# The sum of phi(k) moves from Pool to a column-tiled batch on PE, layernorm is applied six tiles behind, and each output tile starts with its attention part

## The chip, the core and the metric

The kernel runs on one core of a Trainium2 chip. The metric is the device time in microseconds of one execution, as a median over runs. Engines are named as in the profile: PE (matrix multiply), PEld (its weight loads), DVE (vector), ACT (activation), POOL (GpSimd), SP (issues most of the DMA).

## The reference

x has 2048 rows (positions) of 512 features, in bf16. Attention has 32 heads of 16 features. One gate value per row mixes the two branches.

```
g = sigmoid((x * gate_w).sum(-1, keepdims=True))
# branch A, linear attention
q, k, v = split_heads(x @ wqkv)
phi = lambda t: where(t > 0, t + 1, exp(t)) + 1e-6
pq, pk = phi(q), phi(k)
kv = einsum("bhsd,bhse->bhde", pk, v);  z = einsum("bhsd->bhd", pk)
a = merge_heads((pq @ kv) / (pq . z + 1e-6)) @ wo
# branch B, token-mixing MLP on h = layernorm(x) over the features
u = gelu(einsum("bsd,sf->bdf", h, w1) + b1)       # F = 1792
b = transpose(einsum("bdf,fs->bds", u, w2) + b2)
out = g * a + (1 - g) * b
```

## The kernel before

The 2048 rows are 16 tiles of 128. The program is one fixed order per engine: each engine takes its instructions in the order in which the code issues them, and waits on semaphores where operands come from another engine or from a DMA. All PSUM tiles come from one pool of 8 banks of 128x512 fp32; a bank is reused when its last reader is done.

- **K stage** (lines 252 to 272, to about 47 us). For each tile t: `k_tiles` multiplies the transposed tile by the k weights (4 matmuls into `kacc`); `phi` makes phi(k) from it with an Exp on ACT (`e`), a min-and-add on DVE (`e` in place) and a max-and-add on DVE (`pk`). A POOL add then sums `pk` into `zacc` (line 211), which later gives z. `g_tile(t-2)` adds x^T phi(k) of an earlier tile into four banks `gacc` (4 matmuls); kv follows from it and the v weights later. Tiles 0 to 7 are transposed on PE (4 small matmuls each) and copied to `xT` by DVE or ACT; tiles 8 to 15 come transposed by DMA. Beside this runs the layernorm of branch B: `ln_stats` (two DVE instructions per tile, `stats` and `mv`); for each group of four tiles `ln_rstd` (a DVE add `veps`, a POOL power `rstd`) and `ln_shift` (DVE, `nmr`); and `ln_apply` (one ACT instruction per tile writes `hs`). `ln_apply` runs four tiles behind: that of tile 0 stands on ACT behind the Exp of tile 4 and ahead of those of tiles 5 and later.
- **q stage** (lines 332 to 345, to about 78 us). Sixteen steps: 3 matmuls of `uacc` (the first three column blocks of w1) and 4 of `qacc`, whose phi is again one ACT and two DVE instructions. The last tiles of `ln_apply` and the evictions of `gacc` to `gT` run at its start. Inside stand `kv_matmuls` (step 4; it also turns `zacc` into the columns `Z32` that the denominator needs) and `w2_matmuls` (step 8).
- **u stage** (to about 114 us): the other 11 column blocks of w1, 16 matmuls each. `den_matmuls` (16 matmuls of 32 columns, on four column groups of the array), a reciprocal, and a chain of DMAs and DVE multiplications that scales `pqT`.
- **Output stage** (lines 393 to 415): for each row tile 14 matmuls of branch B (`yps`), ACT scales them by 1 - g and adds the bias (`b_sc`), 4 matmuls of branch A (`aps`), and DVE adds g times these (`ot`); SP stores the tile. The last tile's attention part goes in two halves of 256 columns.

Of the kernel before, what the change touches and what calls it, by code (L numbers as in the profile page):

```python
# [15 lines left out]
def kernel(  # L16
# [13 lines left out]
    nc = tc.nc  # L30
    P = nc.NUM_PARTITIONS
# [27 lines left out]
    work = ctx.enter_context(tc.tile_pool(name="work", bufs=3))  # L59
# [17 lines left out]
    pqT = keep([P, ND, S], BF16, "pqT")  # L77
    pk = keep([P, NT, D], BF16, "pk")
    uT = keep([P, NF, D], BF16, "uT")
    kvbdT = keep([P, ND, P], BF16, "kvbdT")  # L80
    W2sb = keep([P, ND, D], BF16, "W2sb")
    Z32 = keep([P, ND, 32], BF16, "Z32")
    zacc = keep([P, D], FP32, "zacc")
    zcol = keep([P, ND], FP32, "zcol")
    rden = keep([P, SC], BF16, "rden")
    ident = keep([P, P], BF16, "ident")
# [11 lines left out]
    gg = keep([P, NT], FP32, "gg")  # L98
    c1 = keep([P, NT], FP32, "c1")
    c2 = keep([P, NT], FP32, "c2")  # L100
    mhalf = keep([P, TPC], FP32, "mhalf")
    ones_f = keep([P, 1], FP32, "ones_f")
    warm = keep([P, SC], BF16, "warm")

    def mm(o, lhsT, rhs, start, stop, **kw):
        nc.tensor.matmul(o, lhsT=lhsT, rhs=rhs, start=start, stop=stop, **kw)  # L106
# [56 lines left out]
    )  # L163
    block_mask(mask[:].rearrange("p (a b) -> p a b", b=HEAD), P // HEAD, HEAD)
    block_mask(maskH[:].rearrange("p (a b) -> p a b", b=1), 8, 1)
    nc.gpsimd.memset(zacc[:], 0.0)
    nc.gpsimd.dma_start(out=brow[0:NF, :], in_=B_b1.rearrange("(f q) -> f q", q=P))
    nc.gpsimd.dma_start(out=brow[NF : NF + NT, :], in_=B_b2.rearrange("(f q) -> f q", q=P))
    nc.gpsimd.dma_start(
        out=gw_b[:], in_=gate_w.rearrange("(o d) -> o d", o=1).to_broadcast([P, D])  # L170
# [12 lines left out]
    def transpose_tile(t, on_act):  # L183
        pt = bank("pt", BF16)
        for k in range(ND):
            nc.tensor.transpose(pt[:, k * P : (k + 1) * P], xs[:, t, k * P : (k + 1) * P], ident[:])
        dst = xT[:, :, t * P : (t + 1) * P]
        src = pt[:].rearrange("p (k s) -> p k s", k=ND)
        if on_act:
            nc.scalar.activation(out=dst, in_=src, func=ACT.Copy)  # L190
        else:
            nc.vector.tensor_copy(out=dst, in_=src)
# [8 lines left out]
            out=dst, in0=acc[:], scalar=0.0, in1=e[:], op0=ALU.max, op1=ALU.add  # L201
        )

    def k_tiles(ts):
        accs = [bank("kacc") for _ in ts]
        for k in range(ND):
            for t, acc in zip(ts, accs):
                mm(acc[:], xT[:, k, t * P : (t + 1) * P], wk_sb[:, k, :], k == 0, k == ND - 1)
        for t, acc in zip(ts, accs):
            phi(pk[:, t, :], acc)  # L210
            nc.gpsimd.tensor_tensor(out=zacc[:], in0=zacc[:], in1=pk[:, t, :], op=ALU.add)  # L211

    def ln_stats(t):
        stats = work.tile([P, nc.vector.BN_STATS_DIM], FP32, name="stats", tag="stats", bufs=2)
        nc.vector.bn_stats(out=stats[:], in_=xs[:, t, :])  # L215
        nc.vector.bn_aggr(out=mv[:, t, :], in_=stats[:])  # L216

    def ln_rstd(g):
        s = slice(g * TPC, (g + 1) * TPC)
        nc.vector.tensor_scalar_add(out=veps[:, s], in0=mv[:, s, 1], scalar1=EPS)  # L220
        nc.gpsimd.tensor_tensor(out=rstd[:, s], in0=veps[:, s], in1=mhalf[:], op=ALU.pow)  # L221

    def ln_shift(g):
        s = slice(g * TPC, (g + 1) * TPC)
# [13 lines left out]
    def g_tile(t):  # L238
        for k in range(ND):
            mm(gacc[k][:], xs[:, t, k * P : (k + 1) * P], pk[:, t, :], t == 0, t == NT - 1)  # L240

    def q_block(i):
        c, j = divmod(i, ND)
        qacc = bank("qacc")
        for k in range(ND):
            mm(
                qacc[:], wq_sb[:, k, j * P : (j + 1) * P], xT[:, k, c * SC : (c + 1) * SC],
                k == 0, k == ND - 1,
            )
        phi(pqT[:, j, c * SC : (c + 1) * SC], qacc)  # L250

    transpose_tile(0, False)
    transpose_tile(1, False)
    warm_up(2, 256)
    k_tiles((0, 1))
    transpose_tile(2, True)
    transpose_tile(3, True)
    LAG = 2
    for t in range(2, NT + LAG):
        if t < NT:  # L260
            k_tiles((t,))
        if 4 <= t + 2 < 8:
            transpose_tile(t + 2, True)
        g_tile(t - LAG)
        if t % TPC == 0 and t <= NT:
            ln_shift(t // TPC - 1)
        if TPC <= t:
            ln_apply(t - TPC)
        for u in (0, 1, 2) if t == 2 else (t,) if t < NT else ():
            ln_stats(u)  # L270
            if u % TPC == TPC - 1:
                ln_rstd(u // TPC)

    gT = persist.tile([P, ND, D], BF16, name="gT", tag="wk_sb")
    for k in range(ND):
        if k % 2:
            nc.vector.tensor_copy(out=gT[:, k, :], in_=gacc[k][:])
        else:
            nc.scalar.activation(out=gT[:, k, :], in_=gacc[k][:], func=ACT.Copy)
    for t in range(NT + LAG - TPC, NT):  # L280
        ln_apply(t)

    def gelu(j, acc):
        nc.scalar.activation(  # L284
# [9 lines left out]
    def kv_matmuls():  # L294
        kvps = bank("kvps")
        for j in range(ND):
            for k in range(ND):
                mm(
                    kvps[:, j * P : (j + 1) * P], wv_sb[:, k, j * P : (j + 1) * P],
                    gT[:, k, j * P : (j + 1) * P], k == 0, k == ND - 1,  # L300
                )
        nc.vector.tensor_tensor(
            out=kvbdT[:], in0=kvps[:].rearrange("p (j d) -> p j d", j=ND),
            in1=mask[:].unsqueeze(1).to_broadcast([P, ND, P]), op=ALU.mult,
        )
        zps = bank("zps")
        for j in range(ND):
            mm(zps[:, j : j + 1], zacc[:, j * P : (j + 1) * P], ones_f[:], True, True)
        nc.vector.tensor_copy(out=zcol[:], in_=zps[:, 0:ND])
        for j in range(ND):  # L310
            nc.vector.tensor_scalar_mul(
                out=Z32[:, j, 8 * j : 8 * j + 8], in0=maskH[:], scalar1=zcol[:, j : j + 1]
            )
# [51 lines left out]
    w2c = []  # L365
# [6 lines left out]
    for j in range(NB0, NF):  # L372
        c, jj = divmod(j, FB)
# [18 lines left out]

    for t in range(NT):
        c, tl = divmod(t, TPC)
        yps = bank("yps")
        for f in range(NF):
            mm(yps[:], w2c[c][:, f, tl * P : (tl + 1) * P], uT[:, f, :], f == 0, f == NF - 1)
        b_sc = work.tile([P, D], FP32, name="b_sc", tag="b_sc", bufs=2)
        nc.scalar.activation(  # L399
            out=b_sc[:], in_=yps[:], func=ACT.Identity,  # L400
            scale=c1[:, t : t + 1], bias=c2[:, t : t + 1],
        )
        halves = 2 if t == NT - 1 else 1
        W = D // halves
        for h in range(halves):
            cs = slice(h * W, (h + 1) * W)
            aps = bank("aps")
            for j in range(ND):
                mm(aps[:, :W], pqT[:, j, t * P : (t + 1) * P], W2sb[:, j, cs], j == 0, j == ND - 1)
            ot = opool.tile([P, D], BF16, name="ot", tag="ot")  # L410
            nc.vector.scalar_tensor_tensor(  # L411
                out=ot[:, :W], in0=aps[:, :W], scalar=gg[:, t : t + 1], in1=b_sc[:, cs],
                op0=ALU.mult, op1=ALU.add,
            )
            nc.sync.dma_start(out=o_view[:, t, cs], in_=ot[:, :W])

# [29 lines left out]
```

## Time and profile before

| What | Value |
|---|---|
| median of 3 runs (lowest, highest) | 183.13 us (183.01, 184.39) |
| the profiled execution | 182.21 us, span 180.2 us |
| mean granted TensorE clock | 0.987 |
| busy: PE, DVE, ACT, POOL | 165.0, 89.5, 57.5, 36.9 us |

The span runs from the first to the last instruction that the profiler saw; the rest of the 182.21 us lies around it. A granted clock of 1.00 is the higher of TensorE's two levels, 2.4 GHz, and 0.50 the lower, 1.2 GHz. Matmul ends are modelled, so pitches (start to start) are used for matmul durations.

### The profile page before, as it was taken

What the parts mean: (1) busy time and instruction counts of PE and PEld (TensorE: products, weight loads), DVE (VectorE), ACT (ScalarE), POOL (GpSimd) and SP (SyncE); (2) the same over time, 40 slices, a digit from 0 to 9 for tenths busy, and PEclk for the clock granted to TensorE, in tenths of its full rate; (3) what the DMA queues carried; (4) which work ended last, traced back from release to release, by engine and by line L of the source; (5) the groups of instructions that cost most, each with busy time, mean ns of one, the idle gap of its engine ahead of it and who ended that gap; (6) DMA issues with size and microseconds to landing.
All of it is one profiled execution on the core that took longest, in us unless ns stands there. A gap on an engine that the chain in (4) does not pass through costs nothing.

```text
span 180.2 us, 2109 instructions
## 1 busy us (share of the span) xinstructions
PE 165.0 (92%) x792; PEld 74.6 (41%) x792; DVE 89.5 (50%) x192; ACT 57.5 (32%) x90; POOL 36.9 (20%) x53
## 2 busy tenths in 40 slices
PE   7799597884799999999999999999999999999991
PEld 3354133331346444444444444444444444444440
DVE  1489898988739787699901141204411111311111
ACT  3442745527192323561121131103311122111121
POOL 7275454574500000000063234200000000000000
PEclk9999969999999999999999999999999999999998
DMA  5999999996000000029019949996211000011100
GB/s 154 334 206 230 363 349 348 347 338 161 0 0 4 2 0 0 0 77 328 6 62 284 253 128 298 235 308 156 87 33 60 30 29 29 29 33 50 38 29 29
DMA packets 27866, 24.53 MB, mean 136 GB/s; under 512 B 5648, under 2 KB 27280, under 8 KB 27856
## 3 DMA queue, kind: packets, MB, share of 16 engines
q1 hardware_dynamic: 25984, 21.63, 40.9%
q0 software_dynamic: 1440, 2.38, 5.7%
q10 hardware_dynamic: 432, 0.39, 0.7%
q8 instruction: 6, 0.10, 0.3%
q14 instruction: 4, 0.03, 0.1%
HBM read 21.11 MB, written 2.23 MB: 130 GB/s over the span
## 4 chain that ended last, share of the span: by engine, by line
PE 70%; DVE 17%; ACT 4%; DMA 2%; POOL 2%; issue 1%; SPq 0%; DVEq 0%
PE yps L106 27%; PE uacc L106 26%; PE qacc L106 7%; PE aps L106 7%; DVE stats L215 4%; DVE pk L200 4%; DVE e L197 3%; DMA wk_sb<-in_A_wqkv_dram 2%; POOL rstd L221 2%; ACT e L196 2%; DVE nmr L225 2%; DVE mv L216 1%; ACT hs L231 1%; DVE veps L220 1%; PE kacc L106 1%
## 5 line engine op out<-in xcount | busy, mean ns | idle before, releaser
L106 PE MATMUL uacc<-hs,w1c 128*128 128x512 bf16 x224 | 51.3, 379 | 0.0
L106 PE MATMUL yps<-uT,w2c 128*128 128x512 bf16 x224 | 51.0, 379 | 0.0
L106 PEld LDWEIGHTS <-w2c 128*128 128x128 bf16 x224 | 21.9, 98 | 26.5
L106 PEld LDWEIGHTS <-w1c 128*128 128x128 bf16 x224 | 21.8, 98 | 26.2 <-issue 0.4
L411 DVE SCALAR_TENSOR_TENSOR ot<-aps,gg,b_sc 128x512 bf16<-128x512 f32 (+1 forms) x17 | 12.1, 719 | 40.9 <-PE aps L106 36.7
L399 ACT ACTIVATE b_sc<-yps,c,c 128x512 f32<-128x512 f32 x16 | 12.3, 777 | 49.0 <-PE yps L106 39.4
L106 PE MATMUL gacc<-pk,xs 128*128 128x512 bf16 x64 | 17.3, 394 | 6.4 <-DVE pk L200 6.3
L211 POOL TENSOR_TENSOR zacc<-zacc,pk 128x512 f32<-128x512 f32 x16 | 18.4, 1153 | 20.5 <-DVE pk L200 20.4
L106 PE MATMUL kacc<-wk_sb,xT 128*128 128x512 bf16 x64 | 17.4, 395 | 3.3 <-ACT xT L190 3.1
L363 DVE TENSOR_TENSOR pqT<-pqT,rex 128x512 bf16<-128x512 bf16 x16 | 6.7, 425 | 27.3 <-DMA rex<-rd_dram 27.2
L231 ACT ACTIVATE hs<-xs,nmr,rstd 128x512 bf16<-128x512 bf16 x16 | 12.7, 809 | 18.2 <-DVE nmr L225 18.2
L197 DVE TENSOR_SCALAR e<-e 128x512 bf16<-128x512 bf16 x32 | 12.5, 391 | 11.9 <-ACT e L196 11.9
L284 ACT ACTIVATE uT<-uacc,bcol 128x512 bf16<-128x512 f32 x14 | 9.3, 687 | 28.6 <-PE uacc L106 28.6
L106 PE MATMUL qacc<-xT,wq_sb 128*128 128x512 bf16 x64 | 16.4, 379 | 0.4 <-DVE pqT L200 0.2
L106 PE MATMUL aps<-W2sb,pqT 128*128 128x512 bf16 (+1 forms) x68 | 16.4, 367 | 0.0
L196 ACT ACTIVATE e<-qacc 128x512 bf16<-128x512 f32 x16 | 9.2, 597 | 13.8 <-PE qacc L106 12.9
L361 POOL DMA_DIRECT2D rex<-rd_dram x16 | 9.4, 594 | 16.6 <-DVE pqT L363 14.8
L106 PEld LDWEIGHTS <-xs 128*128 128x128 bf16 x64 | 6.2, 100 | 15.0 <-issue 9.8
L196 ACT ACTIVATE e<-kacc 128x512 bf16<-128x512 f32 x16 | 9.3, 588 | 7.0 <-PE kacc L106 7.0
L200 DVE SCALAR_TENSOR_TENSOR pk<-kacc,e 128x512 bf16<-128x512 f32 x16 | 11.1, 692 | 0.6
L200 DVE SCALAR_TENSOR_TENSOR pqT<-qacc,e 128x512 bf16<-128x512 f32 x16 | 11.1, 692 | 0.6
L106 PEld LDWEIGHTS <-xT 128*128 128x128 bf16 x64 | 6.2, 101 | 11.9 <-ACT xT L190 3.8
(61 smaller groups left out, 87.4 us busy)
## 6 DMA issues: line engine op xcount, KB each, us to landing
w2c<-in_B_w_dram SPq DMA_DIRECT2D x4, 1792.0 KB, 10.8
w1c<-in_B_w_dram SPq DMA_DIRECT2D x2, 2048.0 KB, 16.9
w1c<-in_B_w_dram SPq DMA_DIRECT2D x3, 1024.0 KB, 9.2
rex<-rd_dram POOLq DMA_DIRECT2D x16, 128.0 KB, 6.9
out_dram<-ot SPq DMA_DIRECT2D x15, 128.0 KB, 1.7
xs<-in_A_x_dram SPq DMA_DIRECT2D x3, 512.0 KB, 8.1
wq_sb<-in_A_wqkv_dram SPq DMA_DIRECT2D x1, 512.0 KB, 4.4
wv_sb<-in_A_wqkv_dram SPq DMA_DIRECT2D x1, 512.0 KB, 11.2
```

What stands on the lines that cost most here:

```text
L106: nc.tensor.matmul(o, lhsT=lhsT, rhs=rhs, start=start, stop=stop, **kw)
L196: nc.scalar.activation(out=e[:], in_=acc[:], func=ACT.Exp)
L197: nc.vector.tensor_scalar(out=e[:], in0=e[:], scalar1=1.0, scalar2=PHI_EPS, op0=ALU.min, op1=ALU.add)
L200: nc.vector.scalar_tensor_tensor(out=dst, in0=acc[:], scalar=0.0, in1=e[:], op0=ALU.max, op1=ALU.add)
L211: nc.gpsimd.tensor_tensor(out=zacc[:], in0=zacc[:], in1=pk[:, t, :], op=ALU.add)
L215: nc.vector.bn_stats(out=stats[:], in_=xs[:, t, :])
L231: nc.scalar.activation(out=hs[:, t, :], in_=xs[:, t, :], func=ACT.Identity, scale=rstd[:, t : t + 1], bias=nmr[:, t : t + 1],)
L284: nc.scalar.activation(out=uT[:, j, :], in_=acc[:], func=ACT.Gelu_apprx_tanh, bias=bcol[:, j : j + 1])
L361: nc.gpsimd.dma_start(out=rex[:], in_=src.unsqueeze(1).to_broadcast([8, HEAD, SC]))
L363: nc.vector.tensor_tensor(out=seg, in0=seg, in1=rex[:], op=ALU.mult)
L399: nc.scalar.activation(out=b_sc[:], in_=yps[:], func=ACT.Identity, scale=c1[:, t : t + 1], bias=c2[:, t : t + 1],)
L411: nc.vector.scalar_tensor_tensor(out=ot[:, :W], in0=aps[:, :W], scalar=gg[:, t : t + 1], in1=b_sc[:, cs], op0=ALU.mult, op1=ALU.add,)
```

## The change

1. The 16 POOL adds into `zacc` (and its memset) go. Instead a new `z_tile(t)` multiplies `pk` of tile t by a 128x32 matrix `zsel`, whose first column is ones, in one of four column groups of the array; the 16 of them stand at the end of the K stage, 15 ahead of the last `g_tile` and one behind it. DVE copies the result to `zsb`, which takes the place of `zacc`.
2. `ln_apply` goes six tiles behind in place of four, `ln_shift` is issued a tile later and behind `ln_stats` of its tile, and the layernorm of tiles 12 to 15 moves into the q stage (statistics in steps 2 to 5, apply in steps 8 to 11). The statistics of tiles 0 and 1 move ahead of the first `k_tiles`.
3. Tiles 2 and 3 are transposed and copied ahead of the first phi, tile 2 by DVE and not by ACT.
4. In the output stage the attention part comes first: `aps`, then ACT writes `a_sc` (scaled by g, with the bias), then `yps`, and DVE adds 1 - g times these. The last tile splits `yps` and not `aps` in halves.

```diff
-            nc.gpsimd.tensor_tensor(out=zacc[:], in0=zacc[:], in1=pk[:, t, :], op=ALU.add)
+    def z_tile(t):
+        g = t % 4
+        mm(
+            zacc[32 * g : 32 * g + 32, :], zsel[:], pk[:, t, :], t < 4, t >= NT - 4,
+            tile_position=(0, 32 * g),
+        )
...
-    k_tiles((0, 1))
-    transpose_tile(2, True)
-    transpose_tile(3, True)
+    ln_stats(0)
+    ln_stats(1)
+    k_tiles((0, 1), lambda: (transpose_tile(2, False), transpose_tile(3, True)))
     LAG = 2
-    for t in range(2, NT + LAG):
-        if t < NT:
-            k_tiles((t,))
+    APPLY = 6
+    for t in range(2, NT):
+        k_tiles((t,))
         if 4 <= t + 2 < 8:
             transpose_tile(t + 2, True)
         g_tile(t - LAG)
-        if t % TPC == 0 and t <= NT:
+        if t >= APPLY:
+            ln_apply(t - APPLY)
+        if t < 12:
+            ln_stats(t)
+            if t % TPC == TPC - 1:
+                ln_rstd(t // TPC)
+        if t % TPC == 1 and t > TPC:
             ln_shift(t // TPC - 1)
...
+    zacc = bank("zacc")
+    g_tile(NT - 2)
+    for t in range(NT - 1):
+        z_tile(t)
+    g_tile(NT - 1)
+    z_tile(NT - 1)
+    ln_apply(10)
+    ln_apply(11)
+    nc.vector.tensor_copy(out=zsb[:], in_=zacc[:])
...
         q_block(t)
+        if 2 <= t < 6:
+            ln_stats(t + 10)
+        if t == 5:
+            ln_rstd(3)
+        if t == 7:
+            ln_shift(3)
+        if 8 <= t < 12:
+            ln_apply(t + 4)
```

Where the instructions stand on the engines, in three places.

ACT, the start of the K stage, before (`e<-kacc` is the Exp of a tile, `xT<-pt` the copy of a transposed tile, `hs` an `ln_apply`):

```order
L196 ACTIVATE e<-kacc 128x512 x2
L190 ACTIVATE xT<-pt 128x4x128 x2
L196 ACTIVATE e<-kacc 128x512
L190 ACTIVATE xT<-pt 128x4x128
L196 ACTIVATE e<-kacc 128x512
L190 ACTIVATE xT<-pt 128x4x128
L196 ACTIVATE e<-kacc 128x512
L190 ACTIVATE xT<-pt 128x4x128
L231 ACTIVATE hs<-xs,nmr,rstd 128x512
L196 ACTIVATE e<-kacc 128x512
L190 ACTIVATE xT<-pt 128x4x128
```

and now:

```order
L192 ACTIVATE xT<-pt 128x4x128
L198 ACTIVATE e<-kacc 128x512 x3
L192 ACTIVATE xT<-pt 128x4x128
L198 ACTIVATE e<-kacc 128x512
L192 ACTIVATE xT<-pt 128x4x128
L198 ACTIVATE e<-kacc 128x512
L192 ACTIVATE xT<-pt 128x4x128
L198 ACTIVATE e<-kacc 128x512
L192 ACTIVATE xT<-pt 128x4x128
L198 ACTIVATE e<-kacc 128x512
L234 ACTIVATE hs<-xs,nmr,rstd 128x512
```

The copy of tile 3 now stands ahead of the first Exp, the copy of tile 2 is gone from ACT, and the first `hs` stands behind the last copy (tile 7) and not ahead of it.

DVE, from the third-last tile to the end of the K stage, before:

```order
L200 SCALAR_TENSOR_TENSOR pk_80<-kacc_443,e_448 128x512
L215 BN_STATS stats_458<-xs_72 128x6
L216 BN_AGGR mv_94<-stats_458 128x2
L197 TENSOR_SCALAR e_466<-e_466 128x512
L200 SCALAR_TENSOR_TENSOR pk_80<-kacc_461,e_466 128x512
L215 BN_STATS stats_476<-xs_72 128x6
L216 BN_AGGR mv_94<-stats_476 128x2
L197 TENSOR_SCALAR e_484<-e_484 128x512
L200 SCALAR_TENSOR_TENSOR pk_80<-kacc_479,e_484 128x512
L215 BN_STATS stats_494<-xs_72 128x6
L216 BN_AGGR mv_94<-stats_494 128x2
L220 TENSOR_SCALAR veps_95<-mv_94 128x4
```

and now:

```order
L202 SCALAR_TENSOR_TENSOR pk_80<-kacc_426,e_431 128x512
L228 SCALAR_TENSOR_TENSOR nmr_98<-mv_95,rstd_97 128x4
L199 TENSOR_SCALAR e_446<-e_446 128x512
L202 SCALAR_TENSOR_TENSOR pk_80<-kacc_441,e_446 128x512
L199 TENSOR_SCALAR e_460<-e_460 128x512
L202 SCALAR_TENSOR_TENSOR pk_80<-kacc_455,e_460 128x512
L291 COPY zsb_85<-zacc_469 128x512
L296 CAST gT_497<-gacc_161 128x512
L296 CAST gT_497<-gacc_163 128x512
```

The statistics of the last four tiles are gone from between the phi of the tiles, and the copy `zsb` stands ahead of the evictions of `gacc`.

POOL, from the first DMA to the chain that scales `pqT`, before:

```order
L167 DMA brow<-in_B_b_dram 14x128
L168 DMA brow<-in_B_b_dram 16x128
L169 DMA gw_b<-in_gate_w_dram 128x512
L211 TENSOR_TENSOR zacc<-zacc,pk 128x512 x4
L221 TENSOR_TENSOR rstd<-veps,mhalf 128x4
L211 TENSOR_TENSOR zacc<-zacc,pk 128x512 x4
L221 TENSOR_TENSOR rstd<-veps,mhalf 128x4
L211 TENSOR_TENSOR zacc<-zacc,pk 128x512 x4
L221 TENSOR_TENSOR rstd<-veps,mhalf 128x4
L211 TENSOR_TENSOR zacc<-zacc,pk 128x512 x4
L221 TENSOR_TENSOR rstd<-veps,mhalf 128x4
L356 DMA rd_dram<-rden 128x512
```

and now:

```order
L169 DMA brow<-in_B_b_dram 14x128
L170 DMA brow<-in_B_b_dram 16x128
L171 DMA gw_b<-in_gate_w_dram 128x512
L224 TENSOR_TENSOR rstd<-veps,mhalf 128x4 x4
L381 DMA rd_dram<-rden 128x512
```

Only the four powers are left on POOL between the first loads and that chain.

## Rows read from the trace of the kernel before

**Rows 1.** Windows: start:end, us, busy of PE, PEld, DVE, ACT, POOL, granted clock, DMA.

```profile
9.70:47.20 37.50, 28.94 (x132) 12.28 (x130) 33.45 (x67) 17.96 (x30) 20.17 (x19) 0.95 0.97 278
47.20:78.50 31.30, 30.90 (x162) 14.55 (x161) 22.52 (x52) 15.73 (x26) 1.38 (x2) 1.00 0.00 1
```

**Rows 2.** Timeline of PE: start, us, instruction, count, idle before and releaser.

```profile
20.81 1.04 PE L106 MATMUL kacc<-wk_sb,xT 128*128 128x512 bf16 x4 [2.15 <-ACT xT L190]
26.83 1.03 PE L106 MATMUL gacc<-pk,xs 128*128 128x512 bf16 x4
...
28.55 1.03 PE L106 MATMUL gacc<-pk,xs 128*128 128x512 bf16 x4
...
41.97 1.02 PE L106 MATMUL gacc<-pk,xs 128*128 128x512 bf16 x4 [1.81 <-DVE pk L200]
...
47.18 0.81 PE L106 MATMUL uacc<-hs,w1c 128*128 128x512 bf16 x3
...
49.67 1.02 PE L106 MATMUL qacc<-xT,wq_sb 128*128 128x512 bf16 x4 [0.18 <-DVE gT L277]
```

**Rows 3.** Timeline of DVE in the K stage.

```profile
23.42 0.69 DVE L215 BATCH_NORM_STATS2 stats<-xs 128x6 f32<-128x512 bf16 x1
...
24.23 0.71 DVE L197 TENSOR_SCALAR e<-e 128x512 bf16<-128x512 bf16 x1
24.98 0.69 DVE L200 SCALAR_TENSOR_TENSOR pk<-kacc,e 128x512 bf16<-128x512 f32 x1
25.59 0.68 DVE L215 BATCH_NORM_STATS2 stats<-xs 128x6 f32<-128x512 bf16 x1
...
26.91 0.28 DVE L197 TENSOR_SCALAR e<-e 128x512 bf16<-128x512 bf16 x1
```

**Rows 4.** Timeline of POOL in the same stretch.

```profile
23.64 1.15 POOL L211 TENSOR_TENSOR zacc<-zacc,pk 128x512 f32<-128x512 f32 x1 [1.02 <-DVE pk L200]
25.81 1.15 POOL L211 TENSOR_TENSOR zacc<-zacc,pk 128x512 f32<-128x512 f32 x1 [1.02 <-DVE pk L200]
```

**Rows 5.** The tile e on DVE, 50 to 75 us: duration ns minimum/median/maximum.

```profile
L197 DVE TENSOR_SCALAR e<-e x15: 283/294/296, 53.3 to 74.3; 128x512 bf16<-128x512 bf16 x15
```

**Rows 6.** Timelines at the start: PE, PEld and ACT.

```profile
7.02 0.62 PE L186 MATMUL pt<-ident,xs 128*128 128x128 bf16 x8
...
9.34 0.33 PEld L186 LDWEIGHTS <-xs 128*128 128x128 bf16 x4 [0.21 <-DMA xs<-in_A_x_dram]
...
6.96 1.08 ACT L196 ACTIVATE e<-kacc 128x512 bf16<-128x512 f32 x2 [3.27 <-PE kacc L106]
7.93 1.09 ACT L190 ACTIVATE xT<-pt 128x512 bf16<-128x512 bf16 x2
```

**Rows 7.** Timeline of PE around the denominator's batch.

```profile
78.48 1.05 PE L106 MATMUL denps<-pqT,Z 128*32 128x512 bf16 x16
79.46 2.77 PE L106 MATMUL uacc<-hs,w1c 128*128 128x512 bf16 x12
```

**Rows 8.** The first loads of w1 on SP, and the page's median time to landing.

```profile
15.57 1.12 SPq L148 DMA_DIRECT2D w1c<-in_B_w_dram  x2
...
w1c<-in_B_w_dram SPq DMA_DIRECT2D x3, 1024.0 KB, 9.2
```

**Rows 9.** Timeline of PE behind w2_matmuls.

```profile
65.01 1.02 PE L106 MATMUL qacc<-xT,wq_sb 128*128 128x512 bf16 x4 [0.23 <-DVE pqT L200]
```

**Rows 10.** Timelines at the end: PE, ACT and DVE.

```profile
172.28 3.19 PE L106 MATMUL yps<-uT,w2c 128*128 128x512 bf16 x14
175.31 1.04 PE L106 MATMUL aps<-W2sb,pqT 128*128 128x256 bf16 x8
...
175.51 0.78 ACT L399 ACTIVATE b_sc<-yps,c,c 128x512 f32<-128x512 f32 x1 [3.11 <-PE yps L106]
...
176.32 0.88 DVE L411 SCALAR_TENSOR_TENSOR ot<-aps,gg,b_sc 128x256 bf16<-128x256 f32 x2 [3.03 <-ACT b_sc L399]
```

**Rows 11.** Windows: the stretch at the lower clock.

```profile
21.90:25.20 3.30, 3.30 (x9) 1.18 (x8) 3.16 (x8) 1.97 (x5) 1.88 (x2) 0.50 1.11 351
```

More of the change, by code (lines that the diff above doesn't have):

```diff
@@ L82 @@
     Z32 = keep([P, ND, 32], BF16, "Z32")
-    zacc = keep([P, D], FP32, "zacc")
+    zsb = keep([P, D], FP32, "zsb")
+    zsel = keep([P, 32], BF16, "zsel")
     zcol = keep([P, ND], FP32, "zcol")
@@ L158 @@
     nc.vector.memset(Z32[:], 0.0)
+    nc.vector.memset(zsel[:], 0.0)
+    nc.vector.memset(zsel[:, 0:1], 1.0)
     nc.gpsimd.memset(ident[:], 0.0)
@@ L165 @@
     block_mask(maskH[:].rearrange("p (a b) -> p a b", b=1), 8, 1)
-    nc.gpsimd.memset(zacc[:], 0.0)
     nc.gpsimd.dma_start(out=brow[0:NF, :], in_=B_b1.rearrange("(f q) -> f q", q=P))
@@ L202, in phi, with k_tiles @@
         )
-    def k_tiles(ts):
+    def k_tiles(ts, between=None):
         accs = [bank("kacc") for _ in ts]
@@ L208, in k_tiles @@
                 mm(acc[:], xT[:, k, t * P : (t + 1) * P], wk_sb[:, k, :], k == 0, k == ND - 1)
+        if between:
+            between()
         for t, acc in zip(ts, accs):
             phi(pk[:, t, :], acc)
-            nc.gpsimd.tensor_tensor(out=zacc[:], in0=zacc[:], in1=pk[:, t, :], op=ALU.add)
     def ln_stats(t):
@@ L264 @@
         g_tile(t - LAG)
-        if t % TPC == 0 and t <= NT:
-            ln_shift(t // TPC - 1)
[L267 to L272, printed above, removed]
+        if t >= APPLY:
[5 more added lines that the diff above has]
+        if t % TPC == 1 and t > TPC:
+            ln_shift(t // TPC - 1)
+    zacc = bank("zacc")
[7 more added lines that the diff above has]
+    nc.vector.tensor_copy(out=zsb[:], in_=zacc[:])
     gT = persist.tile([P, ND, D], BF16, name="gT", tag="wk_sb")
@@ L279 @@
             nc.scalar.activation(out=gT[:, k, :], in_=gacc[k][:], func=ACT.Copy)
-    for t in range(NT + LAG - TPC, NT):
-        ln_apply(t)
     def gelu(j, acc):
@@ L307, in kv_matmuls @@
         for j in range(ND):
-            mm(zps[:, j : j + 1], zacc[:, j * P : (j + 1) * P], ones_f[:], True, True)
+            mm(zps[:, j : j + 1], zsb[:, j * P : (j + 1) * P], ones_f[:], True, True)
         nc.vector.tensor_copy(out=zcol[:], in_=zps[:, 0:ND])
@@ L394 @@
         c, tl = divmod(t, TPC)
[L395 to L398, printed above, removed]
+        aps = bank("aps")
+        for j in range(ND):
+            mm(aps[:], pqT[:, j, t * P : (t + 1) * P], W2sb[:, j, :], j == 0, j == ND - 1)
+        a_sc = work.tile([P, D], FP32, name="a_sc", tag="a_sc", bufs=2)
         nc.scalar.activation(
-            out=b_sc[:], in_=yps[:], func=ACT.Identity,
-            scale=c1[:, t : t + 1], bias=c2[:, t : t + 1],
-        )
-        halves = 2 if t == NT - 1 else 1
-        W = D // halves
-        for h in range(halves):
+            out=a_sc[:], in_=aps[:], func=ACT.Identity,
+            scale=gg[:, t : t + 1], bias=c2[:, t : t + 1],
+        )
+        parts = 2 if t == NT - 1 else 1
+        W = D // parts
+        for h in range(parts):
             cs = slice(h * W, (h + 1) * W)
-            aps = bank("aps")
-            for j in range(ND):
-                mm(aps[:, :W], pqT[:, j, t * P : (t + 1) * P], W2sb[:, j, cs], j == 0, j == ND - 1)
+            yps = bank("yps")
+            for f in range(NF):
+                mm(
+                    yps[:, :W], w2c[c][:, f, tl * P : (tl + 1) * P], uT[:, f, cs],
+                    f == 0, f == NF - 1,
+                )
             ot = opool.tile([P, D], BF16, name="ot", tag="ot")
             nc.vector.scalar_tensor_tensor(
-                out=ot[:, :W], in0=aps[:, :W], scalar=gg[:, t : t + 1], in1=b_sc[:, cs],
+                out=ot[:, :W], in0=yps[:, :W], scalar=c1[:, t : t + 1], in1=a_sc[:, cs],
                 op0=ALU.mult, op1=ALU.add,
```

## The prediction

> **What bounds the kernel now.** Busy times come first: PE is by far the busiest engine, so the question is where it is not busy. Windows cut at the stage borders answer it [rows 1]: in the K stage PE works 28.94 of 37.50 us and DVE 33.45, while in the q stage PE works 30.90 of 31.30; the u and output stages behind it are as full. What can be won lies in the K stage, the rest being PE's own work.
>
> The timeline of PE then shows who holds it there [rows 2]: gacc groups wait for `pk` on DVE (the longest such wait, 1.81 us, is shown), and once PE waits 2.15 us for `xT` from ACT. The latter is `ln_apply` standing on ACT ahead of that copy, waiting for `nmr`. The timeline of DVE shows the pace [rows 3]: from one `stats` to the next is 25.59 - 23.42 = 2.17 us, more than PE needs for its own eight matmuls, 28.55 - 26.83 = 1.72 us [rows 2].
>
> One piece of those 2.17 us is not DVE's own. The in-place `e` takes 0.71 us where a POOL add into `zacc` covers it (24.23, the add from 23.64 to 24.79), and 0.28 us as the add ends beside it (26.91) [rows 3, 4]. In the q stage, where POOL adds nothing, fifteen of them lie between 283 and 296 ns [rows 5]. So an add costs DVE some 0.43 us through `e`, while `stats` and `pk` take the same 0.69 us with it and without.
>
> **The change part by part.**
>
> *POOL adds and DVE's pace.* Without the adds a tile with statistics costs DVE 24.23 - 23.42 = 0.81 (`stats`, `mv`), 0.28 + 0.04 (`e`, and the gap behind it) and 25.59 - 24.98 = 0.61 (`pk`): 1.74 us [rows 3]. Only tiles 2 to 11 have statistics in the loop; tiles 12 to 15 cost 0.93. PE needs 1.72 per tile, and up to step 5 some 0.25 more for a tile's four transposes (eight took 0.62, the last one's modelled tail included) [rows 6]. DVE and PE thus run level over tiles 2 to 11. A `pk` is not wanted at once: between a tile's kacc and its gacc stand two more tiles of kacc and gacc, 3.45 us, against about 0.6 (Exp) + 0.3 + 0.7 for its phi, so about 1.8 us of lag is covered. I take PE as the bound, with no wait for DVE; were the cover gone, DVE's excess would show one for one.
>
> *Layernorm six tiles behind.* `ln_apply` of tile 0 now stands behind the Exp of tile 6 and behind the last `xT` copy; its `nmr` is issued at tile 5, behind a POOL power started at tile 3. The 2.15 us wait for `xT` goes, and with it the fall to the lower clock that came right after [rows 2, 11].
>
> *The start.* Transposes of tiles 2 and 3 end at 7.64; ACT's copy of tile 3 takes a slot of 0.5, so the first Exp starts at about 8.2 where it began at 6.96, and `pk` of tile 0 is done at 8.2 + 0.6 + 0.3 + 0.7 = 9.8 [rows 3, 5, 6]. That is when gacc begins. Tile 2's kacc may start earlier than before, but that gains nothing: tile 4's transposes follow it on PE and wait for their x rows, which arrive at 9.34 [rows 6]. From 9.8 on PE has 16 gacc and 13 kacc groups of 1.72 / 2 = 0.86, 24.9 us, three transposed tiles, 0.7, and the new batch. The two statistics that move ahead of the first kacc, and the memsets of `zsel`, lie where DVE waits for PE and for the first phi: 0.
>
> *The batch on PE.* The nearest row is the denominator's: 16 matmuls of 32 columns on four groups take 79.46 - 78.48 = 0.98 us [rows 7], four rounds of 0.215 (a quarter of 0.86) with 0.12 left for going in and out. The new batch is 15 matmuls, four rounds, then one more behind the last gacc: 5 x 0.215 + 2 x 0.12 = 1.32 us. Bounds: 1.08 without the in and out, and 16 x 0.215 + 0.24 = 3.68 if the groups do not overlap. I take 1.32, since shapes and groups are as in the row. The Trainium skill (TensorEngine Tiling (Array Packing), Key Properties) says that changing the tiling mode drains TensorE, which speaks against entering the mode twice. By that rule the two extra changes cost something, without it nothing: the batch would be 1.32 or 1.08 us, and the 0.12 us of rows 7 leave room for the rule and for little more.
>
> So the K stage ends at 9.8 + 24.9 + 0.7 + 1.32 = 36.7, where before the first uacc came at 47.18 [rows 2]: **-10.5 us**.
>
> *What then is late next.* The q stage needs w1's first blocks: two loads issued from 15.57 to 16.7, landing 9.2 us later by the median, some 26 [rows 8]; SP's queue holds no wait on the K stage, so the loads keep their times. DVE copies `zsb` (0.7) ahead of its two `gT` evictions, but the first two `qacc` take banks that ACT frees; ACT has no `hs` left to do there, so the 0.18 us wait for `gT` [rows 2] goes: **-0.2 us**.
>
> *Statistics and apply in the q stage.* A step is 7 matmuls, 1.51 us; DVE's phi needs 0.93, and steps 2 to 5 add 0.81 each. DVE falls behind by 0.23 a step, and by the `kvbdT` and `Z32` work of step 4, and is level again at step 8, where the 0.23 us wait behind w2_matmuls [rows 9] stays as it is. `hs` of tile 12 comes at step 8 and is read at step 12. Cost 0; with five banks for `qacc` the worst is the added DVE work less its slack, 4 x 0.81 - 4 x 0.58, about 1 us. Dropping ACT's four `hs` from the start of the stage pays for it at least in part.
>
> *Output order.* All 16 tiles cost PE the same. At the end, before, PE ends yps at 175.31, then ACT `b_sc` to 176.29, then two half `ot` to 177.20 [rows 10]. Now the 0.86 us of aps come first and 28 half-width matmuls of about 0.11 (eight in 1.04) take 3.1 where 14 took 3.03: PE ends at about 175.31 + 0.86 + 0.2 = 176.4, one half `ot` of 0.44 follows: 176.85. **-0.35 us**. ACT's first `a_sc` waits for g and the bias product as `b_sc` did, and as many banks are held meanwhile; aps needs `pqT` one yps group sooner, but of its first quarter only, which the chain scales first: 0.
>
> Sum: -10.5 - 0.2 - 0.35 = **-11.05 us**. The profiled execution was 182.21 us, so 171.2; the median of the runs shown is 0.92 above it, and there the forecast is 183.13 - 11.05 = **172.1**.
>
> **The rivals.**
>
> *The batch does not overlap.* 3.68 in place of 1.32: 174.5. For it: its weights are the same tile each time, while the denominator's differ; against it: rows 7. Chance 0.06.
>
> *The clock falls once.* Between 7 and 10 us PE still has gaps (up to 9.34 for x, to 9.8 for `pk`). The shown fall came after a 2.15 us gap, and in it 9 matmuls took 3.30 us, which at 0.215 would be 1.94: +1.4, 173.5 [rows 2, 11]. Against it: the mean clock of 0.95 over the K stage is what that one stretch at 0.50 makes, so the gap of 1.81 passed without one [rows 1, 2]. Chance 0.09.
>
> *DVE stays the bound* because `e` is slow in the K stage for another reason, DMA traffic say. Then only the six statistics that leave the loop count: 47.18 - 6 x 0.81 + 0.34 for the last batch matmul = 42.7, or 178.0. Against it: `e` at 0.28 in the same stage [rows 3]. Chance 0.05.
>
> *Slower: the clock stays low.* If PE's early gaps leave it at 1.2 GHz for the stage, each matmul costs 3.30/9 = 0.37 and not 0.215; 116 matmuls (29 groups of four) lose 18 us, giving 190 [rows 11]. It turns the sign from some 71 matmuls on, 26 us at the lower level. The trace has one such stretch and PE came back with work at hand. Chance 0.02.
>
> **How the numbers follow.** The forecast has 0.78, with about 0.8 us either way for lag between engines that I could not see. Cases above 174.8 hold about 0.1 and those below 171.0 some 0.07, so 171.0 to 174.8 is the range; its top takes in the first two rivals. One per cent, 1.8 us, is about what a measurement of this kernel can tell from no change. Every case but the last is faster by more; partial losses of the last kind between give 0.02 to no change.
>
> **What would show it.** `e` on DVE at 0.28 to 0.30 throughout the K stage; gacc and kacc groups in a row at 1.72 per tile from about 10 us, with no wait for `pk`; the first uacc at 36 to 37.5; the first 15 matmuls of `zacc` in about 1 us; granted clock 1.00 from 5 us on; the q stage 31 us long. Waits of gacc for `pk` past tile 4, or a first uacc later than 38, would make the sum wrong; a q stage above 32 would say that the moved statistics found no cover.

## The result, and the profile after

| What | Before | After |
|---|---|---|
| median (lowest, highest) | 183.07 us (182.3, 184.39), 4 runs | 171.81 us (171.37, 172.34), 4 runs |
| ratio of the two, 95% interval | | 0.9379 [0.9319, 0.944] |
| the profiled execution, its span | 182.21, 180.2 us | 172.34, 170.3 us |
| start of the first gacc group | 9.69 us | 10.80 us |
| K stage, first gacc to first uacc | 37.49 us | 27.21 us |
| q stage, to the denominator's batch | 31.30 us | 30.96 us |
| u stage, to the first output matmul | 35.53 us | 35.53 us |
| first output matmul to the end of the last `ot` | 63.19 us | 62.87 us |

The change makes the kernel 11.26 us faster by the medians. The stages of the two profiled executions add up to 1.11 - 10.28 - 0.34 + 0 - 0.32 = -9.83 us, and those executions stand 9.87 us apart. Nearly all of the gain is in the K stage, and the start of the profiled execution of after gives 1.1 us back. The ratios here and below use undisturbed runs: one run of spare_adds took 351.63 us and counts in its median of 174.98, but not in its ratio.

The windows of after, cut at the same borders as [rows 1] (start:end, us, busy of PE, PEld, DVE, ACT, POOL, granted clock, DMA):

```profile
10.80:38.00 27.20, 27.04 (x141) 12.26 (x144) 22.26 (x56) 18.96 (x31) 3.06 (x3) 1.00 1.11 307
38.00:68.90 30.90, 30.51 (x155) 14.57 (x157) 25.72 (x61) 15.24 (x25) 1.08 (x1) 1.00 0.23 64
```

In the K stage PE is now busy 27.04 of 27.20 us where it was busy 28.94 of 37.50, and DVE has 5 us to spare. POOL went from 20.17 to 3.06 us. The granted clock is 1.00 in both stages. The view of waits for this stretch (engine, line, waited for: total us, times, longest) has one wait of PE's matmuls left, the one ahead of the first gacc:

```profile
PE gacc L107 <- DVE pk L202: 0.7, 1, 0.7
```

The timeline of PE, from the start over the middle to the end of the stage and on to the last tile, answers to [rows 2, 7, 9, 10]:

```profile
7.10 1.02 PE L107 MATMUL kacc<-wk_sb,xT 128*128 128x512 bf16 x4 [0.23 <-DMA wk_sb<-in_A_wqkv_dram]
7.96 0.61 PE L188 MATMUL pt<-ident,xs 128*128 128x128 bf16 x8
...
10.80 1.04 PE L107 MATMUL gacc<-pk,xs 128*128 128x512 bf16 x4 [0.68 <-DVE pk L202]
...
18.39 1.03 PE L107 MATMUL gacc<-pk,xs 128*128 128x512 bf16 x4
...
20.11 1.03 PE L107 MATMUL gacc<-pk,xs 128*128 128x512 bf16 x4
...
35.75 1.04 PE L107 MATMUL zacc<-pk,zsel 128*32 128x512 bf16 x15
36.72 1.04 PE L107 MATMUL gacc<-pk,xs 128*128 128x512 bf16 x4
37.69 0.39 PE L107 MATMUL zacc<-pk,zsel 128*32 128x512 bf16 x1
38.01 0.82 PE L107 MATMUL uacc<-hs,w1c 128*128 128x512 bf16 x3
...
55.50 1.02 PE L107 MATMUL qacc<-xT,wq_sb 128*128 128x512 bf16 x4 [0.23 <-DVE pqT L202]
...
68.97 1.05 PE L107 MATMUL denps<-pqT,Z 128*32 128x512 bf16 x16
...
163.63 3.22 PE L107 MATMUL yps<-uT,w2c 128*128 128x256 bf16 x28
```

From one gacc group to the next it is 20.11 - 18.39 = 1.72 us, PE's own pace. The batch of 15 takes 36.72 - 35.75 = 0.97 us, the single matmul behind the last gacc 38.01 - 37.69 = 0.32, and that last gacc itself 0.97 where a group takes 0.86. The timeline of DVE shows the pace beside it, to be compared with [rows 3]:

```profile
20.15 0.68 DVE L218 BATCH_NORM_STATS2 stats<-xs 128x6 f32<-128x512 bf16 x1
...
20.97 0.27 DVE L199 TENSOR_SCALAR e<-e 128x512 bf16<-128x512 bf16 x1
21.27 0.69 DVE L202 SCALAR_TENSOR_TENSOR pk<-kacc,e 128x512 bf16<-128x512 f32 x1
21.88 0.68 DVE L218 BATCH_NORM_STATS2 stats<-xs 128x6 f32<-128x512 bf16 x1
```

From `stats` to `stats` it is 1.73 us where it was 2.17, and `e` takes 0.27 where it took 0.71. Over the whole execution its 32 instances average 286 ns, by the page's row (busy us, mean ns | idle before):

```profile
L199 DVE TENSOR_SCALAR e<-e 128x512 bf16<-128x512 bf16 x32 | 9.2, 286 | 7.0 <-ACT e L198 6.8
```

### The profile page after: what moved, and what is told of

Same layout as the page of the kernel before. It is cut to its first block, busy times and chain, and to the rows that moved or that the text cites. A ratio compares the mean times of both kernels' runs of the same rounds, so it can differ in the third digit from the quotient of the medians.

```text
span 170.3 us, 2113 instructions
## 1 busy us (share of the span) xinstructions
PE 163.1 (96%) x803; PEld 76.0 (45%) x818; DVE 82.7 (49%) x196; ACT 58.2 (34%) x89; POOL 18.0 (11%) x36
## 4 chain that ended last, share of the span: by engine, by line
PE 90%; DMA 3%; ACT 2%; DVE 1%; issue 1%; SPq 0%
PE yps L107 28%; PE uacc L107 28%; PE gacc L107 8%; PE aps L107 8%; PE qacc L107 8%; PE kacc L107 7%; DMA wk_sb<-in_A_wqkv_dram 3%; ACT e L198 1%; PE zacc L107 1%; PE pt L188 1%; PE denps L107 1%; PE kvps L107 1%; PE zps L107 0%; ACT hs L234 0%; DVE pk L202 0%
## 5 line engine op out<-in xcount | busy, mean ns | idle before, releaser
L107 PE MATMUL uacc<-hs,w1c 128*128 128x512 bf16 x219 | 50.7, 379 | 0.4 <-issue 0.2
L107 PE MATMUL yps<-uT,w2c 128*128 128x512 bf16 (+1 forms) x234 | 50.6, 366 | 0.2
L107 PEld LDWEIGHTS <-w2c 128*128 128x128 bf16 x238 | 23.3, 98 | 25.3
L439 DVE SCALAR_TENSOR_TENSOR ot<-yps,c,a_sc 128x512 bf16<-128x512 f32 (+1 forms) x17 | 12.1, 719 | 38.8 <-PE yps L107 37.7
L424 ACT ACTIVATE a_sc<-aps,c,gg 128x512 f32<-128x512 f32 x16 | 12.2, 778 | 46.9 <-PE aps L107 35.6
L107 PE MATMUL gacc<-pk,xs 128*128 128x512 bf16 x62 | 16.0, 379 | 0.7 <-DVE pk L202 0.7
L107 PE MATMUL aps<-W2sb,pqT 128*128 128x512 bf16 x63 | 16.4, 379 | 0.1
L199 DVE TENSOR_SCALAR e<-e 128x512 bf16<-128x512 bf16 x32 | 9.2, 286 | 7.0 <-ACT e L198 6.8
L218 DVE BATCH_NORM_STATS2 stats<-xs 128x6 f32<-128x512 bf16 x16 | 10.9, 682 | 0.0
L374 DVE CUSTOM_DVE_ANT_0 junk<-xs,gw_b 128x512 bf16<-128x512 bf16 x16 | 9.9, 684 | 0.0
```

What stands on the lines that cost most here:

```text
L199: nc.vector.tensor_scalar(out=e[:], in0=e[:], scalar1=1.0, scalar2=PHI_EPS, op0=ALU.min, op1=ALU.add)
L374: nc.vector.tensor_tensor_reduce(out=junk[:], in0=xs[:, t, :], in1=gw_b[:], scale=1.0, scalar=0.0, op0=ALU.mult, op1=ALU.add, accum_out=gp ...
L424: nc.scalar.activation(out=a_sc[:], in_=aps[:], func=ACT.Identity, scale=gg[:, t : t + 1], bias=c2[:, t : t + 1],)
L439: nc.vector.scalar_tensor_tensor(out=ot[:, :W], in0=yps[:, :W], scalar=c1[:, t : t + 1], in1=a_sc[:, cs], op0=ALU.mult, op1=ALU.add,)
```

## The experiments

The theory was the one of the prediction: POOL's adds slow DVE, and the order around `ln_apply` stalls ACT and PE; without both PE is the bound. The rivals were that one of the two parts carries the gain by itself (the first two runs tell), and that the adds cost DVE nothing as such, so that the gain comes from what waited on them or on their place in the order (the third run tells). All distances "first gacc to first uacc" are from the profiled execution; after has 27.21.

| Label | Median us | Ratio to before [95%] | First gacc to first uacc, us |
|---|---|---|---|
| z_only | 176.3 | 0.9617 [0.9573, 0.966] | 30.92 |
| adds_on_pool | 174.49 | 0.9524 [0.9478, 0.9569] | 30.14 |
| spare_adds | 174.98 | 0.9548 [0.9482, 0.9613] | 30.56 |
| lag_back | 173.5 | 0.9481 [0.9431, 0.9532] | 29.04 |
| stats_back | 171.51 | 0.938 [0.9326, 0.9434] | 27.21 |
| no_stats | 171.72 | 0.9388 [0.9342, 0.9434] | 27.21 |
| one_group | 173.79 | 0.9506 [0.946, 0.9552] | 29.58 |
| old_output | 172.06 | 0.9382 [0.9338, 0.9427] | 27.21 |
| start | 170.82 | 0.9311 [0.9268, 0.9354] | 27.20 |
| best | 170.28 | 0.9277 [0.923, 0.9324] | 27.21 |

### Each part alone

**z_only** is the kernel before with the batch in place of the POOL adds, and nothing else:

```diff
-            nc.gpsimd.tensor_tensor(out=zacc[:], in0=zacc[:], in1=pk[:, t, :], op=ALU.add)
...
+        if t == NT + 1:
+            zacc = bank("zacc")
+            for u in range(NT - 1):
+                z_tile(u)
         g_tile(t - LAG)
+        if t == NT + 1:
+            z_tile(NT - 1)
+            nc.vector.tensor_copy(out=zsb[:], in_=zacc[:])
```

> The kernel before with one part of the change: the sum of phi(k) as the batch on PE, no adds on POOL; layernorm, transposes and output order stay as they were. Theory (the adds cost DVE 0.43 us per tile through e, and the layernorm order is a second, smaller cost): e on DVE at 0.28 to 0.30, nmr and veps near 0.16, so DVE needs about 1.74 us a tile with all 16 statistics in the loop; the wait of ACT for nmr ahead of the copy of xT shrinks but does not vanish; first uacc at 39 to 41, time 175 to 177. Rival A (the gain is the layernorm order that blocked ACT, the adds cost nothing): time 181 to 183.

**adds_on_pool** is the reverse: after, with the adds on POOL and no batch:

```diff
+            nc.gpsimd.tensor_tensor(out=zsb[:], in0=zsb[:], in1=pk[:, t, :], op=ALU.add)
...
-    for t in range(NT - 1):
-        z_tile(t)
     g_tile(NT - 1)
-    z_tile(NT - 1)
```

> The changed kernel with the adds on POOL as before and no batch on PE; all moves of layernorm, transposes and output order are kept. Theory: e back at about 0.7 us, 2.17 us of DVE for each of ten tiles and 1.36 for four, first uacc near 42, time 176.5 to 178. Rival A: first uacc near 36.5 to 38, time 170.5 to 172, the batch's 1.3 us on PE being saved.

The first part alone brings 6.8 us, the moves alone 8.6, both together 11.3: neither is idle, and the two overlap by 4 us. z_only came where it was expected; adds_on_pool was 2 us faster than its range. DVE's pace was not what the expectation had wrong: in adds_on_pool the `stats` from tile 3 on follow one another at 2.17 to 2.25 us, against 2.17 expected. But ten tiles of 2.17 us and four of 1.36 are 27.1 us, and from `e` of tile 2, which begins at 11.36, they end at 38.5 (the last `pk` ends at 39.79); with one gacc group behind them that is a first uacc near 39.4, and not 42. How the 42 was worked out is not on record. The first uacc of before less six statistics, 47.18 - 6 x 0.81 = 42.3, would give it, and would keep the stall that the moves take away.

What is left in each is different. In z_only, the waits from first gacc to first uacc:

```profile
ACT hs L232 <- DVE nmr L226: 8.4, 3, 3.2
...
PE gacc L107 <- DVE pk L202: 2.3, 3, 0.9
PEld L107 <- ACT xT L192: 1.0, 1, 1.0
...
PE kacc L107 <- ACT xT L192: 0.6, 1, 0.6
```

In adds_on_pool, the window of the stage and the same view:

```profile
10.60:40.70 30.10, 26.96 (x128) 11.96 (x129) 28.01 (x57) 17.97 (x30) 21.08 (x19) 1.00 1.10 309
...
PE gacc L106 <- DVE pk L200: 3.7, 8, 1.0
```

In z_only PE's matmuls wait 2.9 us in this view (PEld's 1.0 us is the same stall as kacc's 0.6). Matmul ends are modelled; by starts, with 0.865 us for a group, PE loses 3.7 us, which is the 3.71 by which its stage is longer than after's. DVE has no POOL add to fight; what stands in the way is `hs` on ACT, which waits for `nmr` three times with the next Exps and copies queued behind it. In adds_on_pool that order is mended, and DVE is busy 28.01 of 30.10 us: its pace holds seven gacc groups for 3.0 us in this view (the first of the eight waits, 0.7 us, lies ahead of the stage), and for 4.4 us by starts. So either cure leaves the other stall, and with both gone PE's own work is the floor.

The two stalls are also not separate, which bears on the 4 us. In before a POOL add starts just ahead of `nmr` and holds it to the end; in z_only `nmr` is short. The timelines of DVE and POOL in before, then DVE in z_only:

```profile
28.13 1.11 DVE L225 SCALAR_TENSOR_TENSOR nmr<-mv,rstd 128x4 f32<-128x4 f32 x1 [0.21 <-POOL rstd L221]
...
28.07 1.15 POOL L211 TENSOR_TENSOR zacc<-zacc,pk 128x512 f32<-128x512 f32 x1
...
24.89 0.16 DVE L226 SCALAR_TENSOR_TENSOR nmr<-mv,rstd 128x4 f32<-128x4 f32 x1 [0.20 <-POOL rstd L222]
```

In the K stage of before ACT waits 13.2 us for `nmr`, in z_only 8.4. Taking the adds away thus also shortens the wait that the moves take away. How much of the 4 us is this, and how much the floor, no run separates. Nor are the 8.6 us the order on ACT alone: the moves also take six tiles' statistics out of the loop, which counts while DVE is the bound, as it is with the adds. No run has the adds and only one of the moves.

### The adds as such

**spare_adds** is after, batch and all, with 16 adds on POOL whose result nobody reads (the buffer is the space of `uT`, which is written later):

```diff
+    scratch = uT[:, 0:2, :].bitcast(FP32).rearrange("p a b -> p (a b)")
+    nc.gpsimd.memset(scratch, 0.0)
...
             phi(pk[:, t, :], acc)
+            nc.gpsimd.tensor_tensor(out=scratch, in0=scratch, in1=pk[:, t, :], op=ALU.add)
```

> The changed kernel, with batch and all, and beside it the same 16 POOL adds into a buffer that nobody reads: nothing waits for their result. Theory (the adds slow DVE by running beside it): e at about 0.7 us and POOL's powers behind the adds, first uacc near 42 to 43, time 177 to 178.5. Rival B (the adds cost by what waits for them, the power that stands behind them on POOL): e stays at 0.28, time within 0.7 us of the changed kernel's 171.8.

174.98 us: 3.2 us slower than after, with no reader to wait for the adds. The rival is refuted. The range of the theory was 2 us too high, and here too it is the 42 to 43 for the first uacc, which comes at 40.65, and not DVE's pace. The timelines of DVE and POOL in spare_adds:

```profile
19.88 0.58 DVE L231 SCALAR_TENSOR_TENSOR nmr<-mv,rstd 128x4 f32<-128x4 f32 x1
20.38 0.28 DVE L201 TENSOR_SCALAR e<-e 128x512 bf16<-128x512 bf16 x1
...
22.12 0.71 DVE L201 TENSOR_SCALAR e<-e 128x512 bf16<-128x512 bf16 x1
...
19.29 1.16 POOL L217 TENSOR_TENSOR uT<-uT,pk 128x512 f32<-128x512 f32 x1 [1.02 <-DVE pk L204]
21.53 1.16 POOL L217 TENSOR_TENSOR uT<-uT,pk 128x512 f32<-128x512 f32 x1 [1.09 <-DVE pk L204]
```

The first add runs to 20.45, and `nmr` (0.16 without an add, in z_only above) begins under it and ends at 20.46; the `e` behind it takes 0.28. The second runs to 22.69, and here it is `e` that takes 0.71 and ends at 22.83. Of the two that an add can hold here, the one that comes first pays, and the other runs at its short time.

### Layernorm's order

**lag_back** is after with `ln_shift` and `ln_apply` four tiles behind, as before; statistics and all else stay:

```diff
+        if t % TPC == 0:
+            ln_shift(t // TPC - 1)
+        if t >= TPC:
+            ln_apply(t - TPC)
...
-        if t >= APPLY:
-            ln_apply(t - APPLY)
```

> The changed kernel with one part undone: layernorm is applied four tiles behind again, and the shift is issued at the head of each group of four, as before; adds stay off POOL, the last four tiles' statistics stay in the q stage. Theory (the order on ACT and DVE is the second cost: ACT waits for nmr ahead of an Exp and ahead of one xT copy): waits of ACT for nmr of 1.5 to 3 us come back at tiles 4 and 8, PE waits 0.5 to 1 us for xT and as much for pk, time 172.8 to 174.5. Rival E (once the adds are gone, the lag is worth nothing): 171.6 to 172.2.

173.5 us, in its range, and the stage is 1.83 us longer. That is half of the 3.71 us between z_only and after; the rest lies in the other moves (statistics, transposes), which no run takes back together with the lag. The timelines of ACT and PE in lag_back:

```profile
24.48 0.81 ACT L234 ACTIVATE hs<-xs,nmr,rstd 128x512 bf16<-128x512 bf16 x1 [2.27 <-DVE nmr L228]
...
35.00 1.02 PE L107 MATMUL gacc<-pk,xs 128*128 128x512 bf16 x4 [0.86 <-DVE pk L202]
```

ACT waits for `nmr` three times (6.5 us in all), and PE feels it later as a wait for `pk`; the wait for `xT` that was expected beside it, as in [rows 2], did not come.

**stats_back** is after with the statistics of tiles 12 to 15 in the K loop again; **no_stats** is after without the statistics of tiles 2 to 11 at all, with ones in their place:

```diff
-        if t < 12:
-            ln_stats(t)
-            if t % TPC == TPC - 1:
-                ln_rstd(t // TPC)
+        ln_stats(t)
+        if t % TPC == TPC - 1:
+            ln_rstd(t // TPC)
```

```diff
+    nc.vector.memset(mv[:], 1.0)
...
         if t < 12:
-            ln_stats(t)
             if t % TPC == TPC - 1:
```

> The changed kernel with one part undone: the statistics of tiles 12 to 15 stay in the K stage's loop (and POOL's last power with them); everything else as changed. Theory (PE is the bound now and DVE level with it, phi having 1.8 us of slack): DVE fills the idle time of tiles 12 to 15, gacc waits little, first uacc 0 to 0.6 us later, time 171.8 to 172.5. Rival D (DVE still sets the pace, so each statistic counts): 4 x 0.81 = 3.2 us, time near 175.

> The changed kernel without the statistics of tiles 2 to 11: their 20 DVE instructions, 8.1 us, are left out, and the layernorm of these tiles goes by constants. Theory (PE is the bound): first uacc within 0.2 us of the changed kernel's counted from the first gacc (27.2), time 171.4 to 172.0. Rival D: DVE has 0.93 us a tile to do, the stage gets 2 us shorter or more.

Their windows of the K stage, stats_back first:

```profile
10.00:37.20 27.20, 27.20 (x144) 12.29 (x144) 25.20 (x65) 18.96 (x31) 3.66 (x4) 1.00 1.10 313
```

```profile
10.20:37.40 27.20, 27.20 (x144) 12.24 (x145) 14.96 (x36) 18.84 (x31) 3.12 (x3) 1.00 1.10 314
```

DVE works 25.20 us in one and 14.96 in the other, against 22.26 in after, and the stage is 27.2 us in all three. DVE is no longer the bound there, and moving the last four tiles' statistics out of the stage brought nothing once the adds were gone. The time of stats_back, 171.51 us, lies 0.3 below its range.

### The batch and the other end

**one_group** is after with all 16 matmuls of the batch in one column group:

```diff
-            zacc[32 * g : 32 * g + 32, :], zsel[:], pk[:, t, :], t < 4, t >= NT - 4,
-            tile_position=(0, 32 * g),
+            zacc[0:32, :], zsel[:], pk[:, t, :], t == 0, t == NT - 1,
+            tile_position=(0, 0),
```

> The changed kernel with all 16 matmuls of the batch in one column group of the array in place of four; DVE copies the 32 rows of it. This prices the overlap of the groups. Theory: 16 x 0.215 in place of 0.97 + 0.32, the batch of 15 takes 3.2 us, time 174.0 to 174.4. Rival F (the matmuls of one group overlap as well, or the batch lies beside something that ends later): under 0.7 us more.

```profile
34.72 3.41 PE L107 MATMUL zacc<-pk,zsel 128*32 128x512 bf16 x15
38.06 1.04 PE L107 MATMUL gacc<-pk,xs 128*128 128x512 bf16 x4
```

In this timeline of PE in one_group the 15 take 38.06 - 34.72 = 3.34 us, where four groups take 0.97. The stage grows by the same 2.37 us and the time by 2.0, to 0.2 us under its range.

**old_output** is after with the output stage of before (the MLP part first, the last tile's attention part in halves):

```diff
-        aps = bank("aps")
...
+        yps = bank("yps")
+        for f in range(NF):
+            mm(yps[:], w2c[c][:, f, tl * P : (tl + 1) * P], uT[:, f, :], f == 0, f == NF - 1)
+        b_sc = work.tile([P, D], FP32, name="b_sc", tag="b_sc", bufs=2)
```

> The changed kernel with the output stage in its old order, branch B's part first and the last attention part in halves. Theory: only the end differs, the last half tile is ready 0.35 us later, time 172.1 to 172.2, within what three rounds can tell. Rival C (the order of the parts matters at the start of the stage too, where ACT waits for g): 1 us or more.

It is 0.25 us above after by the medians, less than the intervals can part. The traces show this part of the change better: from first output matmul to the end of the last `ot` it is 63.19 us in old_output, as in before, and 62.87 in after.

### The start, and a faster version

**start** is after with one thing changed: on ACT the Exp of tile 0 stands ahead of the copy of tile 3, so that `pk` of tile 0 need not wait for that copy.

```diff
-        if between:
-            between()
+        pt = between() if between else None
         for t, acc in zip(ts, accs):
             phi(pk[:, t, :], acc)
+            if pt is not None and t == 0:
+                later(pt)
```

> The changed kernel with one order on ACT changed: the Exp of tile 0 stands ahead of the copy of transposed tile 3, which stands ahead of the Exp of tile 1. Theory (the first gacc comes 2.84 us behind the last kacc of tile 1, because that copy holds the first Exp back): the distance falls to about 2.1, time 0.5 to 0.8 us lower, 171.0 to 171.3. Rival G (PE waits there for tile 4's rows of x anyway): within 0.2 us.

The timelines of ACT and PE in start:

```profile
7.58 0.60 ACT L202 ACTIVATE e<-kacc 128x512 bf16<-128x512 f32 x1 [3.86 <-PE kacc L107]
8.24 0.60 ACT L196 ACTIVATE xT<-pt 128x512 bf16<-128x512 bf16 x1
...
7.59 0.61 PE L188 MATMUL pt<-ident,xs 128*128 128x128 bf16 x8
...
9.60 1.03 PE L107 MATMUL gacc<-pk,xs 128*128 128x512 bf16 x4
```

From those transposes to the first gacc it is 2.01 us, where after needs 10.80 - 7.96 = 2.84, and no wait for `pk` is left ahead of the first gacc. The time is 170.82 us, 1.0 below after and 0.2 under its range; the intervals of the two ratios overlap, so it is the trace that shows the gain.

**best** adds two small things: the four W2 matmuls go one to a step in steps 8 to 11, not four into step 8, and the last tile is split 384 to 128, not in halves.

```diff
-        if t == 8:
-            w2_matmuls()
+        if 8 <= t < 12:
+            w2_matmuls((t - 8,))
...
+        for cs in (slice(0, 384), slice(384, D)) if t == NT - 1 else (slice(0, D),):
```

> As the run before, and two small edits more: the four W2 matmuls go one each into steps 8 to 11 of the q stage, and the last output tile is split 384 and 128 columns. Theory: the wait of 0.23 us for a bank behind w2_matmuls goes (0.2 to 0.4 us), the last ot is 0.15 us shorter; together with the first Exp 0.8 to 1.3 us under the changed kernel, 170.5 to 171.0.

170.28 us, 0.2 under its range and the lowest median of all, below both kernels. The q stage is 30.57 us where start has 30.96, 0.23 of it the wait behind w2_matmuls, which is gone, and the output takes 62.75 against 62.88. By the medians best is 0.54 us below start, with intervals of the ratios that overlap; the traces' 0.39 and 0.13 add up to the same.

## Why the prediction held, step by step

**The K stage.** The forecast had 36.7 us for the first uacc and the trace 38.01. Of the 1.3 us between them 1.0 is the start: gacc was forecast for 9.8 and begins at 10.80. The distance from the transposes of tiles 2 and 3 to the first gacc came out as worked, 2.84 us against 2.78; but those transposes begin at 7.96 and not at 7.02 [rows 6], because the kacc ahead of them waits for a load of `wk_sb` (7.10 in the timeline above; the slowest of these loads lands 5.3 us after its issue, where it took 4.3 in before). In the other kernels with this start the first gacc lies between 9.77 and 10.57, so I read 10.80 as the late end of what that load does from run to run, and the forecast's 9.8 as its early end. That load's landing is not shown to be due to the change. The rest, 0.3, is PE's own work being a little longer: 27.21 us against 24.9 + 0.7 + 1.32 = 26.92. The sum was said to be wrong from a first uacc past 38; 38.01 is just past that mark, through the start and not through the stage.

**DVE's pace.** That `e` would fall to 0.28 and DVE run level with PE over tiles 2 to 11 was right, and spare_adds shows that the adds as such were the cause. The prediction priced an add at 0.43 us through `e` and said nothing of `veps` and `nmr`, which the adds hold as well: `veps` takes 0.47 us in before and 0.17 in z_only, `nmr` 1.11 and 0.16, and ACT waits for `nmr`. The forecast counted on 1.8 us of lag as cover; no_stats shows that even 7 us less of DVE's work in the stage would bring nothing more.

**The wait of `ln_apply`** was rightly taken as a loss of its own: lag_back puts it at 1.7 us of the time in a kernel without the adds. With them it is longer: ACT waits 13.2 us for `nmr` in the K stage of before and 8.4 in z_only; the prediction put this wait down to the order alone. The fall to the lower clock that followed the wait in before [rows 2, 11] is not in the K stage of after or of any of the experiments: granted clock 1.00 in each.

**The batch.** 0.97 + 0.32 + 0.11 (on the last gacc) = 1.40 us against 1.32. The rival in which the groups do not overlap is refuted by the 0.97 us; one_group, which is that case, takes 173.79 against the 174.5 worked out for it. Going in and out of the batch costs little: the batch and its two neighbours stand 1.40 - 5 x 0.215 = 0.33 us above the bare rounds. The rule of the Trainium skill weighed there (TensorEngine Tiling (Array Packing), Key Properties), that a change of tiling mode drains TensorE, has no price on that page. The 0.33 us agree with the rule, and no run separates a drain from other causes.

**Late next.** Nothing was: the q stage went from 31.30 to 30.96 (forecast -0.2, measured -0.34), the moved statistics cost nothing there, and the 0.23 us wait behind w2_matmuls stayed, as said. The tail was forecast at -0.35 and measures -0.32.

**The other rivals.** The clock did not fall in the early gaps, DVE did not stay the bound, and nothing went slower.

The forecast of 172.1 thus was met by 171.81, to which luck added something. The profiled execution of after is at 172.34, which the sum puts at 171.2, and the 1.1 us between is mostly the start. The medians hide this: that of before lies 0.86 us above its profiled execution, that of after 0.53 below.

## What to carry to other kernels

Two stalls on one stage do not add up: work out the floor that the busiest engine sets (here 27.2 us), and price each cure by how far it brings the stage to that floor with the other stall still in place. An add on an idle engine is not free if it holds another engine that is near its bound; look for an instruction whose duration varies between two values, and for what ends when the long one ends. On an in-order engine an instruction that waits for a far chain (`hs` for `nmr`) delays what is queued behind it, so place it where its operand is long done.

## What the runs showed of the hardware

A POOL add does not slow all that DVE does beside it: it holds an `e`, `veps` or `nmr` that meets it until about its own end. In the kernel before, `e` from 24.23 to 24.94 lies across the end of an add at 24.79 [rows 3, 4], and `nmr` from 28.13 to 29.24 covers almost a whole add that ends at 29.22; in spare_adds it was `nmr` in one place and `e` in the next. Each ends 0.01 to 0.15 us after the add. What an add costs thus depends on where it is met: 0.43 us for an `e` that begins 0.59 us into it, 0.95 for the `nmr` that begins 0.06 us into it. `stats` (0.68) and `pk` (0.69) keep their durations under an add. The Trainium skill says of the port pair that DVE and GpSimd share that it is an exclusive lock for the whole instruction, and that the loser blocks fully (SBUF — State Buffer, Terms); these rows agree for the DVE instructions that are held.

Column groups of the array work side by side: 15 matmuls of 32 columns, with the same weights each time, take 0.97 us on four groups and 3.34 us on one.
